# Pooling the first two batches' keys and values on TensorE, with a new lead-in order

## The chip, the cores and the metric

The kernel runs on one core of a Trainium2 chip. The metric is the device time of one execution in microseconds (us). Engines are named as in the profile: PE is TensorE (matmuls; PEld is its weight loads), DVE is VectorE, ACT is ScalarE, POOL is GpSimd, SP is SyncE, which issues the DMAs here.

## What is computed

Three stages follow one another on 4608 tokens (8 batches of 576): attention with keys and values averaged over groups of 8 rows, a SoLU layer with a normalization, and a SiLU layer.

```python
# q, k, v: (8 batches, 8 heads, 576, 64), f32
k_p = k.reshape(B, H, Sp, 8, D).mean(axis=3)        # Sp = 72
v_p = v.reshape(B, H, Sp, 8, D).mean(axis=3)
scores = scale * np.matmul(q, k_p.transpose(0, 1, 3, 2))
attn = softmax(scores)
x = np.matmul(attn, v_p)                             # to (4608, 512)
h = x @ w_in                                         # moe: 512 -> 1024
solu = h * softmax(h)
ln = (solu - mean) / np.sqrt(var + 1e-06) * g_ln
x = ln @ w_out                                       # 1024 -> 512
h = x @ w_in2                                        # moe2: 512 -> 2048
out = (h * sigmoid(h)) @ w_out2                      # 2048 -> 512
```

## The kernel before

Tokens are worked in 36 tiles of 128. Attention and the SoLU layer run as a software pipeline over the tiles: one step per tile from step 6 on, in an order of letters (`STEP`), and a lead-in for the first tiles with an order written out by hand (`SCRIPT`). The SiLU layer follows, first its input product, then its output product; the change doesn't touch either.

The letters: `q` loads a tile of queries, `S` makes its scores (`scores`, L311) and the negated maximum on DVE (L320), `X` the softmax (ACT L329, POOL L339 and L345), `T` transposes the probabilities on PE and splits them into a high and a low part (`probs_T`, L364, L369), `A` attends one segment of 256 or 320 tokens (`attend`, L415), `H` is the hidden product of a tile (`hidden1`, L440; `Ht,f,k` one eighth of it), `M`, `E`, `Z` the SoLU and its normalization (L451, L458 and L459, L468 and on), `N` the transposes of the result (L487), `P` the output product (`project1`, L504 and L505). `Bn,u` advances the background work n times, taking up new items whose step is at most u.

Background work is a list of generators, sorted by step. It holds the preparation of keys and values (`prep_k`, `prep_v`, `prep_v_rest`) and of the SoLU weights. The weights come as 64-bit floats: `convert` loads them (L130), scales the high words on ACT (L138) and builds 32-bit floats in three DVE steps (L141, L142, L145); `load_split` then keeps a rounded part (ACT L155) and the rest (POOL L156). There are 8 such pieces of the input weights (`w1i`) and 8 of the output weights (`w1o`).

Keys and values of every batch are laid out on the host so that the 8 rows of a group lie next to each other in a partition. `prep_k` loads a head pair (L236) into one of three shared buffers `raw`, sums the 8 on DVE (L241) and copies the halves into the block-diagonal `kbd` (ACT L246 for batches 0 and 1, POOL L248 later). `prep_v` does the same with the first 64 pooled rows (L256, L261), and splits them into `vbh` (ACT L267) and `vbl` (POOL L268). `prep_v_rest` takes the last 8 pooled rows of each head (L273, L278), which come three times over from the host, and writes them with POOL through a mask into `vls` (L283, L287).

PE's order is the order in which the program is written (`manual_schedule`); the order of ACT, DVE, POOL and SP in these stages is that of a planner, which goes by its own costs and by the program's order. `gps` gives PSUM buffers from a ring of 4.

Of the kernel before, what the change touches and what calls it, by code (L numbers as in the profile page):

```python
# [9 lines left out]
F32 = mybir.dt.float32  # L10
# [3 lines left out]
AF = mybir.ActivationFunctionType  # L14
# [6 lines left out]
POOL = 8  # L21
# [29 lines left out]
NRING = 9  # L51
UNITS = ((0, 1, 2), (3,), (4, 5), (6, 7))
LEAD = 5
EARLY = [4, 5, 6, 7, 9]
W1O, CH0, FIRST = 5, 7, 6
SCRIPT = """
q1 q0 S0 B6,-9 X0 B1,-8 B2,5 S1 B3,-8 q2 B1,2 q3 X1 B2,5 B3,-7 T0 T1 S2 X2 B2,-7 B2,-6 T2
B2,-7 B1,-7 S3 q4 B1,-7 q5 A0 H0,0,0 B1,-6 X3 H0,0,3 B1,2 B1,-7 B3,-7 H0,0,2 S4 B1,9 B6,2
H0,1,3 H0,0,1 H0,1,2 H0,1,0 X4 B1,5 T3 H0,1,1 B1,-6 B1,-7 B1,-6 q6 B2,2 M0 B1,5 E0 B1,-7 S5
Z0 B2,-7 T4 B4,2 H1,0,2 B7,2 A1 B2,5 B1,-7 B1,9 X5 B2,-6 H1,0,0 H1,1,2 H1,0,1 H1,1,1 H1,1,0  # L60
H1,0,3 B3,9 B2,-6 H1,1,3 M1 N0 T5 E1 Z1
"""
STEP = "B2 S H0 A B1 H1 M B1 B1 N E P1 X B3 P T B5 p B1 q B2 Z B1 B2"
TAIL = "H0 A H1 p B2 M N B1 E B2 Z P1 B2 B6 P B2"
# [18 lines left out]
def pooled_attention__solu__silu_kernel(  # L83
    ctx: ExitStack,
    tc: tile.TileContext,
    qT: bass.AP,
    kT: bass.AP,
    vm: bass.AP,
    vl: bass.AP,
# [103 lines left out]
    for i in range(2):  # L193
        nc.gpsimd.memset(kbd[i], 0.0)
        nc.gpsimd.memset(vbh[i].bitcast(F32), 0.0)
        nc.gpsimd.memset(vbl[i].bitcast(F32), 0.0)

    todo, going, ready = [], [], set()
    kept = {"s": 0, "p": 0, "x": 0}

    def add(step, key, items):
        todo.extend((step, key, x) for x in items)
        todo.sort(key=lambda x: x[0])
# [25 lines left out]
                    break  # L229

    raw_t, kp_t, vp_t, vr_t = {}, {}, {}, {}

    def prep_k(b, p):
        assert b < 2 or kept["s"] >= (b - 1) * S
        raw = aw.tile([P, SP, POOL], F32, tag="raw", name="raw", bufs=RAWS)
        nc.sync.dma_start(raw, kT[b, :, p])  # L236
        yield
        if p == 0:
            kp_t[b] = aw.tile([P, NP, SP], F32, tag="kp", name="kp", bufs=1)
        kp, kb = kp_t[b], kbd[b % 2]  # L240
        nc.vector.reduce_sum(kp[:, p], raw, axis=AX)  # L241
        yield
        for e in range(2):
            r = slice(64 * e, 64 * e + 64)
            if b <= 1:
                nc.scalar.activation(kb[r, p, e * SP : (e + 1) * SP], kp[r, p], AF.Copy)  # L246
            elif p == NP - 1:
                nc.gpsimd.tensor_scalar(  # L248
                    kb[r, :, e * SP : (e + 1) * SP], kp[r], 1.0, 0.0, op0=ALU.mult, op1=ALU.add
                )  # L250

    def prep_v(b, p):
        assert b < 2 or kept["x"] >= (b - 1) * S
        i = b % 2
        raw = aw.tile([P, SP, POOL], F32, tag="raw", name="raw", bufs=RAWS)[:, :D]
        nc.sync.dma_start(raw, vm[b, :, p])  # L256
        yield
        if p == 0:
            vp_t[b] = aw.tile([P, NP, D], F32, tag="vp", name="vp", bufs=1)
        vp = vp_t[b]  # L260
        nc.vector.reduce_sum(vp[:, p], raw, axis=AX)  # L261
        yield
        if p == NP - 1:
            for e in range(2):
                r = slice(64 * e, 64 * e + 64)
                hi, lo = vbh[i][r, :, r], vbl[i][r, :, r]
                nc.scalar.activation(hi, vp[r], AF.Copy)  # L267
                nc.gpsimd.tensor_tensor(lo, vp[r], hi.bitcast(F32), op=ALU.subtract)  # L268

    def prep_v_rest(b, g):  # L270
        i = b % 2
        raw = aw.tile([P, SP, POOL], F32, tag="raw", name="raw", bufs=RAWS)[0:96, :D]
        nc.sync.dma_start(raw, vl[b, :, g])  # L273
        yield
        if g == 0:
            vr_t[b] = aw.tile([96, 2, D], F32, tag="vlp", name="vlp", bufs=1)
        vp = vr_t[b]
        nc.vector.reduce_sum(vp[:, g], raw, axis=AX)  # L278
        yield
        if g == 1:  # L280
            vh = aw.tile([96, 2, D], F32R, tag="vlh", name="vlh", bufs=1)
            nc.scalar.activation(vh, vp, AF.Copy)
            nc.gpsimd.tensor_tensor(  # L283
                vh[32:64], vp[32:64], vh[32:64].bitcast(F32), op=ALU.subtract
            )
            for j in range(4):
                nc.gpsimd.tensor_scalar(  # L287
                    vls[i][:, j // 2 :: 2, (j % 2) * D : (j % 2 + 1) * D],
                    vh.bitcast(F32), mask[:, j : j + 1], 0.0, op0=ALU.mult, op1=ALU.add,
                )  # L290
# [690 lines left out]
    def batch_v(b):  # L981
        return [prep_v(b, p) for p in range(NP)] + [prep_v_rest(b, g) for g in range(2)]

    for b in range(1, B):
        j = b // 2
        k0, v0 = (9 * j + 1, 9 * j + 3) if b % 2 else (9 * j - 4, 9 * j - 2)
        for p in range(NP):
            add(k0 + p // 2, ("k", b), [prep_k(b, p)])
        for n, x in enumerate(batch_v(b)):
            add(v0 + n // 2, ("v", b), [x])  # L990
# [36 lines left out]
    def lead_in(script):  # L1027
        for word in script.split():
            what, n = word[0], [int(x) for x in word[1:].split(",") if x]
            if what == "q":  # L1030
                load_q(*n)
            elif what == "S":
                scores(*n)
            elif what == "X":
# [219 lines left out]
```

## Time and profile before

| what | value |
|---|---|
| median of 3 runs | 1362.82 us (1362.54 to 1364.48) |
| the profiled execution | 1365.19 us |
| its span, first to last instruction | 1363.4 us |
| mean granted TensorE clock | 0.975 of full speed |
| PE busy | 1280.6 us |
| DVE busy | 942.7 us |
| ACT busy | 745.8 us |
| POOL busy | 525.3 us |

The busy times are sums over the span. The stages differ: the first 100 us or so are the lead-in and the first steps, until about 600 us the attention and SoLU pipeline runs, and then the SiLU layer.

### The profile page before, as it was taken

Reading aid. Unit: us, or ns where it says so; the run is one execution under the profiler, and the core shown is the slowest. Engines: PE = TensorE matmul, PEld = TensorE weight load, DVE = VectorE, ACT = ScalarE, POOL = GpSimd, SP = SyncE. Lnnn points to the kernel's source line nnn. Section 1 sums busy time; section 2 is a strip of 40 time slices with the busy share of each in tenths; the row PEclk is TensorE's granted clock in tenths of the full one; section 3 lists DMA queues with packets and bytes.
Section 4 is the critical chain, followed back from the end, with each engine's and each line's share of the span. In section 5 each row is a group of like instructions: output and inputs, shape, how many; then the busy total and the mean of one; then the engine's idle time right before and its main releaser. Section 6 shows DMA issues by size and latency. Waiting matters only on the chain.

```text
span 1363.4 us, 22872 instructions
## 1 busy us (share of the span) xinstructions
PE 1280.6 (94%) x8136; PEld 1199.1 (88%) x8136; DVE 942.7 (69%) x1423; ACT 745.8 (55%) x1914; POOL 525.3 (39%) x728
## 2 busy tenths in 40 slices
PE   2579899989999989998999999999999999999998
PEld 2468787878888878887999999999999999999998
DVE  6997567777767665755866666656447887787775
ACT  4675555655655645544666667666544444444342
POOL 5565344344444334332423433333114333343332
PEclk9789999989999989999999999999999999999999
DMA  7645244443443320312577788666895333443421
GB/s 233 202 147 190 82 140 147 130 149 109 121 125 101 108 77 32 123 48 91 204 282 286 250 293 310 235 237 224 332 358 205 115 103 124 156 155 124 154 93 64
DMA packets 108226, 226.94 MB, mean 166 GB/s; under 512 B 9808, under 2 KB 43600, under 8 KB 106576
## 3 DMA queue, kind: packets, MB, share of 16 engines
q1 hardware_dynamic: 104080, 210.80, 46.5%
q10 hardware_dynamic: 4032, 14.68, 2.8%
q8 instruction: 64, 1.05, 0.3%
q14 instruction: 50, 0.41, 0.1%
HBM read 141.56 MB, written 83.89 MB: 165 GB/s over the span
## 4 chain that ended last, share of the span: by engine, by line
PE 61%; DMA 3%; DVE 2%; ACT 2%; POOL 0%; issue 0%; SPq 0%; ACTq 0%; DVEq 0%; POOLq 0%
PE op L928 27%; PE m L710 22%; PE hp L440 4%; PE xp L504 4%; PE xp L505 2%; DMA gd<-ga 1%; PE tp L487 1%; DMA gr<-gd 1%; DMA w2r<-w2if 1%; PE av L415 1%; PE sp L311 1%; DVE w2s L525 1%; DMA x2d<-xo 0%; ACT w2s L561 0%; ACT pr L329 0%
## 5 line engine op out<-in xcount | busy, mean ns | idle before, releaser
L710 PE MATMUL m<-t,w2s 128*128 128x384 f32 x2016 | 355.9, 337 | 12.3 <-ACT u L795 8.0
L710 PEld LDWEIGHTS m<-t,w2s 128*128 128x128 f32 x2016 | 353.0, 190 | 14.9 <-ACT u L795 9.0
L928 PE MATMUL op<-w2o,gt 128*128 128x256 f32 x3024 | 363.0, 283 | 0.0
L928 PEld LDWEIGHTS op<-w2o,gt 128*128 128x128 f32 x3024 | 363.0, 192 | 0.0
L504 PE MATMUL xp<-ln,w1oh 128*128 128x512 f32 x576 | 212.2, 408 | 2.0 <-DVE ln L124 1.9
L525 DVE TENSOR_TENSOR gt<-gr,gt 128x512 fp32r<-128x512 f32 x180 | 165.3, 952 | 68.6 <-ACT gt L905 68.6
L905 ACT ACTIVATE gt<-gr 128x512 fp32r<-128x512 f32 x180 | 103.4, 623 | 149.5 <-DVE gr L525 123.3
L505 PE MATMUL xp<-ln,w1ol 128*128 128x256 f32 x576 | 163.7, 284 | 0.0
L504 PEld LDWEIGHTS xp<-ln,w1oh 128*128 128x128 f32 x576 | 110.3, 192 | 26.9 <-DVE ln L124 2.8
L440 PE MATMUL hp<-w1ih,xTh 128*128 128x512 f32 x288 | 120.2, 417 | 8.2 <-DVE e L459 8.2
L440 PE MATMUL hp<-w1il,xTh 128*128 128x512 f32 x288 | 116.7, 405 | 0.6 <-POOL w1il L156 0.6
L884 POOL TENSOR_TENSOR s<-gr 128x512 f32<-128x512 f32 x36 | 57.8, 1605 | 153.8 <-DMA gr<-gd 81.0
L440 PE MATMUL hp<-w1ih,xTl 128*128 128x512 f32 x288 | 116.6, 405 | 0.0
L329 ACT ACTIVATE pr<-sp,st 128x72 f32<-128x72 f32 x288 | 88.0, 331 | 49.9 <-POOL st L321 49.7
L505 PEld LDWEIGHTS xp<-ln,w1ol 128*128 128x128 f32 x576 | 111.2, 193 | 0.1
L440 PEld LDWEIGHTS hp<-w1ih,xTh 128*128 128x128 f32 x288 | 57.0, 198 | 21.1 <-issue 8.2
L905 ACT ACTIVATE gt<-s 128x512 fp32r<-128x512 f32 x72 | 42.4, 622 | 55.2 <-POOL s L525 52.3
L721 DVE TENSOR_TENSOR gb<-m,u 128x384 f32<-128x384 f32 x48 | 26.7, 556 | 63.0 <-ACT u L775 55.1
L525 POOL TENSOR_TENSOR tt<-x2r 128x768 f32<-128x768 f32 x22 | 44.0, 2002 | 63.3 <-DMA x2r<-x2d 57.7
L440 PEld LDWEIGHTS hp<-w1ih,xTl 128*128 128x128 f32 x288 | 56.3, 196 | 13.2 <-DVE xTl L124 0.6
L440 PEld LDWEIGHTS hp<-w1il,xTh 128*128 128x128 f32 x288 | 56.9, 198 | 11.4 <-POOL w1il L156 0.9
L123 ACT ACTIVATE ln<-tp 128x512 fp32r<-128x512 f32 x72 | 39.3, 596 | 49.5 <-PE tp L487 49.3
(136 smaller groups left out, 2196.7 us busy)
## 6 DMA issues: line engine op xcount, KB each, us to landing
gr<-gd SPq DMA_DIRECT2D x48, 512.0 KB, 6.0
x2r<-x2d SPq DMA_DIRECT2D x12, 1536.0 KB, 7.5
gd<-ga SPq DMA_DIRECT2D x96, 192.0 KB, 2.5
gd<-gb SPq DMA_DIRECT2D x48, 384.0 KB, 3.1
wod<-wo SPq DMA_DIRECT2D x56, 256.0 KB, 2.4
gr<-gd SPq DMA_DIRECT2D x48, 256.0 KB, 5.3
q<-qT SPq DMA_DIRECT2D x36, 256.0 KB, 3.2
raw<-kT SPq DMA_DIRECT2D x32, 288.0 KB, 3.7
```

Source lines behind the costliest of these rows:

```text
L123: nc.scalar.activation(hi, src, AF.Copy)
L311: nc.tensor.matmul(sp[done : done + n, p // 2, (p % 2) * 2 * SP : (p % 2 + 1) * 2 * SP], q[:, p, done : done + n], kbd[b % 2][:, p, :], st ...
L329: behind["ACT"] = nc.scalar.activation(pr[:, g, h], sv[:, g, h], AF.Exp, scale=SCALE, bias=st[:, 0, g, h : h + 1], accum_out=st[:, 1, g, h ...
L440: nc.tensor.matmul(hp[:, f], l, r, start=(n == 1 and m == 0), stop=(n == KC and m == 2))
L504: nc.tensor.matmul(xp, w1oh[:, k, cs], ln[:, k], start=(k == 0), stop=False)
L505: nc.tensor.matmul(xp[:, :GW], w1ol[:, k, cs], ln[:, k, 0], start=False, stop=(k == FC1 - 1))
L525: eng.tensor_tensor(dst, a, b, op=ALU.subtract)
L710: nc.tensor.matmul(to, wt[:, a, o : o + P], tk[:, b, k], start=(start and k == 0 and m == 0), stop=(k == 1 and m == 2), skip_group_check=n ...
L721: eng.tensor_tensor(dst, a, b, op=ALU.add)
L884: nc.gpsimd.tensor_tensor(s1, a21, a22, op=ALU.add)
L905: nc.scalar.activation(ring[n][:, 0], src, AF.Copy)
L928: nc.tensor.matmul(op[:, 256 * h : 256 * h + 256], t[:, l, i, ts], w[:, r], start=(s == i == h == m == 0), stop=(s == NSET - 1 and i == h ...
```

## The change

Keys and values of batches 0 and 1 (`NATURAL = 2`) come from the host in natural rows: `kn` and `vn`, 576 rows of 512 columns a batch. `load_k` and `load_v` bring them into buffers that later hold other tiles (`ln`, `xo`, `e`): 128 rows to a partition set, so that the 8 rows of a group lie in 8 neighbouring partitions. `taps` holds zeros and ones: `every8` sums 8 partitions to one column, `slide` shifts it for accumulation into 64 rows, `last8` is for the last 8 pooled rows. `pool_k` makes 20 matmuls, with the raw rows as stationary operand, and copies the result out of PSUM into `kbd`. `pool_v` makes 8 accumulating matmuls and 4 for the last rows, with the raw rows as moving operand, and splits the result out of PSUM with ACT and DVE. The lead-in's order is new, with four more letters: `k`, `v` load, `K`, `V` pool. The first values are pooled behind the second tile's scores, ahead of the third tile's; the first segment's attention stands ahead of the third tile's transposes. Batches 2 to 7 are prepared as before, from arrays that now begin with batch 2. A cut of the diff:

```diff
+NATURAL = 2
...
 SCRIPT = """
-q1 q0 S0 B6,-9 X0 B1,-8 B2,5 S1 B3,-8 q2 B1,2 q3 X1 B2,5 B3,-7 T0 T1 S2 X2 B2,-7 B2,-6 T2
-B2,-7 B1,-7 S3 q4 B1,-7 q5 A0 H0,0,0 B1,-6 X3 H0,0,3 B1,2 B1,-7 B3,-7 H0,0,2 S4 B1,9 B6,2
-H0,1,3 H0,0,1 H0,1,2 H0,1,0 X4 B1,5 T3 H0,1,1 B1,-6 B1,-7 B1,-6 q6 B2,2 M0 B1,5 E0 B1,-7 S5
-Z0 B2,-7 T4 B4,2 H1,0,2 B7,2 A1 B2,5 B1,-7 B1,9 X5 B2,-6 H1,0,0 H1,1,2 H1,0,1 H1,1,1 H1,1,0
-H1,0,3 B3,9 B2,-6 H1,1,3 M1 N0 T5 E1 Z1
+q0 k0 q1 v0 K0 S0 B1,-7 X0 S1 B1,-7 V0 X1 q2 B1,-7 T0 T1 B1,-7 S2 B2,-7 k1 X2 q3 B2,-6 A0 T2 B2,-6
+H0,0,0 H0,0,1 S3 K1 v1 H0,0,2 X3 H0,0,3 q4 B3,-6 H0,1,0 S4 H0,1,1 X4 T3 H0,1,2 q5 H0,1,3 M0 B2,5
+V1 E0 S5 Z0 B2,5 X5 T4 H1,0,0 H1,0,1 A1 H1,0,2 H1,0,3 B3,5 H1,1,0 H1,1,1 H1,1,2 H1,1,3 M1 q6 B3,5
+N0 T5 E1 Z1 B3,9
 """
...
+    taps = wk.tile([P, 512], F32, tag="sqd", name="taps", bufs=1)
+    nc.gpsimd.memset(taps, 0.0)
+    slide, last8 = taps[:, 0:112], taps[0:64, 112:496].rearrange("p (j r i k) -> p j r i k", j=4, r=3, k=8)
+    every8 = slide[:, 48:64]
+    nc.vector.reduce_sum(every8, ident.rearrange("p (j k) -> p j k", k=8), axis=AX)
+    for j in range(4):
+        nc.gpsimd.tensor_scalar(
+            last8[:, j, :, j], every8[0:64, 0:8].rearrange("p (o k) -> p o k", o=1).to_broadcast([64, 3, 8]),
+            1.0, 0.0, op0=ALU.mult, op1=ALU.add,
+        )
...
+    def load_rows_of(src, b, to):
+        for j in (0, 2):
+            nc.sync.dma_start(
+                to(j, 2), src[b, j * P : (j + 2) * P].rearrange("(j p) d -> p j d", p=P)
+            )
+        nc.sync.dma_start(to(4, 1)[0:64, 0], src[b, 4 * P : S])
+
+    def load_k(b):
+        nat[b] = wk.tile([P, 8, 512], F32, tag="ln", name="nat")
+        load_rows_of(kn, b, lambda j, n: nat[b][:, j : j + n])
+
+    def load_v(b):
+        late = wk.tile([P, 2, 512], F32, tag="e" if b else "xo", name="natv", bufs=2 if b else 1)
+        head = nat[b]
+        nat["v", b] = [head[:, 5], head[:, 6], late[:, 0], late[:, 1], head[0:64, 7]]
+        nc.sync.dma_start(head[:, 5:7], vn[b, 0 : 2 * P].rearrange("(j p) d -> p j d", p=P))
+        nc.sync.dma_start(late, vn[b, 2 * P : 4 * P].rearrange("(j p) d -> p j d", p=P))
+        nc.sync.dma_start(head[0:64, 7], vn[b, 4 * P : S])
+
+    def pool_k(b):
+        kp = gps("kp")[:, : NP * SP].rearrange("p (a k) -> p a k", k=SP)
+        for j in range(5):
+            rows = P if j < 4 else 64
+            for p in range(NP):
+                nc.tensor.matmul(
+                    kp[:, p, 16 * j : 16 * j + rows // 8],
+                    nat[b][0:rows, j, p * P : (p + 1) * P], every8[0:rows, 0 : rows // 8],
+                    start=True, stop=True,
+                )
+        for e in range(2):
+            r = slice(64 * e, 64 * e + 64)
+            to = kbd[b % 2][r, :, e * SP : (e + 1) * SP]
+            if e == 0 or b:
+                nc.scalar.activation(to, kp[r], AF.Copy)
+            else:
+                nc.vector.tensor_copy(to, kp[r])
+        ready.add(("k", b))
+
+    def pool_v(b):
+        i = b % 2
+        vt = nat["v", b]
+        vp = gps("vp")[:, : NP * D].rearrange("p (a d) -> p a d", d=D)
+        for e in range(2):
+            r = slice(64 * e, 64 * e + 64)
+            for j in range(4):
+                nc.tensor.matmul(
+                    vp[r], slide[:, 48 - 16 * j : 112 - 16 * j],
+                    vt[j].rearrange("p (a e d) -> p e a d", e=2, d=D)[:, e],
+                    start=(j == 0), stop=(j == 3),
+                )
+        vr = gps("vr")[0:96]
+        for j in range(4):
+            nc.tensor.matmul(
+                vr.rearrange("p (g j d) -> p j g d", g=2, d=D)[:, j],
+                last8[:, j].rearrange("p r i k -> p (r i k)"),
+                vt[4].rearrange("p (g j d) -> p j g d", g=2, d=D)[:, j],
+                start=True, stop=True,
+            )
+        for e in range(2):
+            r = slice(64 * e, 64 * e + 64)
+            split(vbh[i][r, :, r], vbl[i][r, :, r], vp[r])
+        to = vls[i].rearrange("p a n -> p (a n)")
+        nc.scalar.activation(to, vr, AF.Copy)
+        nc.vector.tensor_tensor(
+            to[32:64], vr[32:64], to[32:64].bitcast(F32), op=ALU.subtract
+        )
+        ready.add(("v", b))
...
         for e in range(2):
             r = slice(64 * e, 64 * e + 64)
-            if b <= 1:
-                nc.scalar.activation(kb[r, p, e * SP : (e + 1) * SP], kp[r, p], AF.Copy)
-            elif p == NP - 1:
+            if p == NP - 1:
...
-    for b in range(1, B):
+    for b in range(NATURAL, B):
...
+            elif what in "kvKV":
+                {"k": load_k, "v": load_v, "K": pool_k, "V": pool_v}[what](*n)
...
-    add(-9, ("k", 0), [prep_k(0, p) for p in range(NP)])
-    add(-8, ("v", 0), batch_v(0))
...
+        "kn": c(k[:NATURAL].transpose(0, 2, 1, 3).reshape(NATURAL, S, DM)),
+        "vn": c(v[:NATURAL].transpose(0, 2, 1, 3).reshape(NATURAL, S, DM)),

```

## Rows read from the trace of the kernel before

**Rows 1.** Page, busy us, share of the span and instructions of each engine.
```profile
PE 1280.6 (94%) x8136; PEld 1199.1 (88%) x8136; DVE 942.7 (69%) x1423; ACT 745.8 (55%) x1914; POOL 525.3 (39%) x728
```

**Rows 2.** Windows: busy us and instructions of each engine in a stretch, granted clock, DMA.
```profile
30.00:40.00 10.00, 0.00 (x0) 0.00 (x0) 9.87 (x12) 5.00 (x23) 5.21 (x7) 0.59 0.55 186
...
0.00:85.30 85.30, 42.08 (x188) 33.62 (x189) 67.24 (x105) 50.86 (x177) 47.77 (x82) 0.86 0.63 202
...
0.00:112.50 112.50, 67.03 (x314) 54.31 (x314) 93.99 (x151) 74.37 (x248) 70.28 (x119) 0.88 0.61 193
...
160.00:300.00 140.00, 131.12 (x728) 112.47 (x728) 100.29 (x177) 81.33 (x276) 60.08 (x132) 0.96 0.43 129
```

**Rows 3.** Waits, 0 to 112 us: total us, times, longest.
```profile
PE pm L364 <- POOL pb L339: 23.0, 5, 13.0
...
PE sp L311 <- ACT kbd L246: 10.1, 2, 9.7
```

**Rows 4.** Groups by line, DVE, 0 to 81 us: busy us, mean ns; idle before.
```profile
L145 DVE SCALAR_TENSOR_TENSOR w<-raw,w 128x512 int32<-128x512 int32 x11 | 12.0, 1094 | 0.1
...
L142 DVE SCALAR_TENSOR_TENSOR w<-w,sign 128x512 int32<-128x512 int32 x12 | 10.7, 892 | 1.4 <-ACT w L138 1.2
...
L141 DVE TENSOR_SCALAR sign<-raw 128x512 int32<-128x512 int32 x12 | 9.1, 759 | 1.9 <-DMA raw<-w1i 1.9
...
L241 DVE TENSOR_REDUCE kp<-raw 128x72 f32<-128x576 f32 x12 | 8.8, 745 | 8.0 <-DMA raw<-kT 8.0
...
L261 DVE TENSOR_REDUCE vp<-raw 128x64 f32<-128x512 f32 x8 | 5.2, 673 | 1.6 <-DMA raw<-vm 1.6
...
L278 DVE TENSOR_REDUCE vlp<-raw 96x64 f32<-96x512 f32 x4 | 2.7, 664 | 0.0
```

**Rows 5.** Timeline, DVE, POOL and PE, 23 to 52 us: start, us, instruction.
```profile
23.52 0.68 DVE L142 SCALAR_TENSOR_TENSOR w<-w,sign 128x512 int32<-128x512 int32 x1
...
28.61 1.84 POOL L287 TENSOR_SCALAR vls<-vlh,mask 96x128 fp32r<-96x128 f32 x4
...
28.83 0.68 DVE L145 SCALAR_TENSOR_TENSOR w<-raw,w 128x512 int32<-128x512 int32 x1
...
29.43 3.75 DVE L141 TENSOR_SCALAR sign<-raw 128x512 int32<-128x512 int32 x1
...
30.42 2.48 POOL L156 TENSOR_TENSOR w1il<-w,w1ih 128x512 fp32r<-128x512 f32 x2
...
38.94 0.41 DVE L141 TENSOR_SCALAR sign<-raw 128x512 int32<-128x512 int32 x1
...
41.64 1.11 PE L364 MATMUL pm<-ident,pb 128*128 128x128 f32 x4 [12.96 <-POOL pb L339]
...
51.89 0.42 DVE L124 TENSOR_TENSOR xTl<-av,xTh 128x256 fp32r<-128x256 f32 x1
```

**Rows 6.** Groups by line, POOL, 0 to 81 us.
```profile
L268 POOL TENSOR_TENSOR vbl<-vp,vbh 64x256 fp32r<-64x256 f32 x4 | 3.4, 858 | 0.1
...
L287 POOL TENSOR_SCALAR vls<-vlh,mask 96x128 fp32r<-96x128 f32 x8 | 3.3, 422 | 0.2
...
L283 POOL TENSOR_TENSOR vlh<-vlp,vlh 32x128 fp32r<-32x128 f32 x2 | 1.3, 648 | 0.2
```

**Rows 7.** Timeline, PE, 25 to 86 us.
```profile
25.15 1.11 PE L364 MATMUL pm<-ident,pb 128*128 128x128 f32 x4 [4.05 <-POOL pb L339]
...
26.63 2.05 PE L311 MATMUL sp<-kbd,q 128*128 128x144 f32 x8
...
79.43 1.03 PE L487 MATMUL tp<-ident,e 128*128 128x128 f32 x8
...
80.95 1.15 PE L311 MATMUL sp<-kbd,q 128*128 128x144 f32 x8
...
85.30 0.47 PE L440 MATMUL hp<-w1ih,xTh 128*128 128x512 f32 x1 [3.20 <-DVE e L459]
```

**Rows 8.** Waits of the SP queue, 0 to 82 us.
```profile
SPq L256 <- DVE kp L241: 10.1, 6, 4.1
```

More of the change, by code (lines that the diff above doesn't have):

```diff
@@ L86, in pooled_attention__solu__silu_kernel @@
     qT: bass.AP,
+    kn: bass.AP,
+    vn: bass.AP,
     kT: bass.AP,
@@ L231, in pooled_attention__solu__silu_kernel @@
     raw_t, kp_t, vp_t, vr_t = {}, {}, {}, {}
+    nat = {}
+    def load_rows_of(src, b, to):
[14 more added lines that the diff above has]
+        nc.sync.dma_start(head[0:64, 7], vn[b, 4 * P : S])
@@ L233, in prep_k @@
     def prep_k(b, p):
-        assert b < 2 or kept["s"] >= (b - 1) * S
+        assert kept["s"] >= (b - 1) * S
         raw = aw.tile([P, SP, POOL], F32, tag="raw", name="raw", bufs=RAWS)
-        nc.sync.dma_start(raw, kT[b, :, p])
+        nc.sync.dma_start(raw, kT[b - NATURAL, :, p])
         yield
@@ L252, in prep_v @@
     def prep_v(b, p):
-        assert b < 2 or kept["x"] >= (b - 1) * S
+        assert kept["x"] >= (b - 1) * S
         i = b % 2
         raw = aw.tile([P, SP, POOL], F32, tag="raw", name="raw", bufs=RAWS)[:, :D]
-        nc.sync.dma_start(raw, vm[b, :, p])
+        nc.sync.dma_start(raw, vm[b - NATURAL, :, p])
         yield
@@ L272, in prep_v_rest @@
         raw = aw.tile([P, SP, POOL], F32, tag="raw", name="raw", bufs=RAWS)[0:96, :D]
-        nc.sync.dma_start(raw, vl[b, :, g])
+        nc.sync.dma_start(raw, vl[b - NATURAL, :, g])
         yield
@@ L1226 @@
         "qT": c(qr.transpose(2, 0, 1, 3)),
-        "kT": c(k.reshape(B, NP, 2, SP, POOL, D).transpose(0, 2, 5, 1, 3, 4).reshape(B, P, NP, SP, POOL)),
-        "vm": c(vr[:, :, :, :64].transpose(0, 2, 3, 1, 5, 4).reshape(B, P, NP, D, POOL)),
+        "kn": c(k[:NATURAL].transpose(0, 2, 1, 3).reshape(NATURAL, S, DM)),
+        "vn": c(v[:NATURAL].transpose(0, 2, 1, 3).reshape(NATURAL, S, DM)),
+        "kT": c(
+            k[NATURAL:].reshape(B - NATURAL, NP, 2, SP, POOL, D).transpose(0, 2, 5, 1, 3, 4)
+            .reshape(B - NATURAL, P, NP, SP, POOL)
+        ),
+        "vm": c(
+            vr[NATURAL:, :, :, :64].transpose(0, 2, 3, 1, 5, 4).reshape(B - NATURAL, P, NP, D, POOL)
+        ),
         "vl": c(
             np.tile(
-                v.reshape(B, 2, 4, SP, POOL, D)[:, :, :, 64:].transpose(0, 2, 3, 1, 5, 4)
-                .reshape(B, 1, 32, 2, D, POOL), (1, 3, 1, 1, 1, 1),
-            ).reshape(B, 96, 2, D, POOL)
+                v[NATURAL:].reshape(B - NATURAL, 2, 4, SP, POOL, D)[:, :, :, 64:].transpose(0, 2, 3, 1, 5, 4)
+                .reshape(B - NATURAL, 1, 32, 2, D, POOL), (1, 3, 1, 1, 1, 1),
+            ).reshape(B - NATURAL, 96, 2, D, POOL)
         ),
```

## Prediction

> **What bounds the kernel now.** I read the profile from the whole to the part: first the engines' busy shares, then busy time by stage, then who waits for whom in the first 112 us, then the instructions of the engine that sets the pace there.
>
> TensorE (PE) is busy 94% of the span [rows 1], and from 160 us on it has 131.12 of 140 us [rows 2]: behind the lead-in nothing but less matmul work would help, and the change takes none away there. In the lead-in it is otherwise. Until 85.30 us, when the first matmul of the third tile's hidden layer starts [rows 7], PE is busy 42.08 us and idle 43.2; VectorE (DVE) is busy 67.24 [rows 2]. From 30 to 40 us PE does nothing at all while DVE is busy 9.87 of 10; from 85.30 to 112.50 DVE is busy 93.99 - 67.24 = 26.75 of 27.2 us [rows 2]. So where the lead-in loses time, DVE is full.
>
> The waits say the same in another form. PE's largest waits are for the probabilities (23.0 us, the longest 13.0) and for the first keys (10.1, of which 9.7 before the first matmul) [rows 3]. POOL writes the probabilities, but they are late because the maximum of that tile stood behind weight conversions on DVE: one `sign` operation there lasts 3.75 us against 0.41 for the same shape elsewhere, while POOL works on the values [rows 5]. The waits end on POOL, ACT or DVE by name; the queue that is full is DVE's.
>
> **What is removed.** Both batches' pooling reductions leave DVE: 8 of keys at 0.745 us, 8 of values at 0.673 and 4 of the last value rows at 0.664 (the key group of [rows 4] has 12 because 4 belong to batch 2 and stay): 5.96 + 5.38 + 2.66 = 14.0 us. POOL loses the low halves and the masking of the values of both batches, 3.4 + 1.3 + 3.3 = 8.0 us [rows 6].
>
> That POOL work also costs DVE. Undisturbed, the three steps of a conversion last 0.41, 0.68 and 0.68 us [rows 5]; in the lead-in they took 9.1 - 12 x 0.41 = 4.2, 10.7 - 12 x 0.68 = 2.5 and 12.0 - 11 x 0.68 = 4.5 us more than that [rows 4], 11.2 in sum. POOL is busy 47.77 us until 85.30 [rows 2], of which some 5 are the first microseconds' memsets, before any conversion. If the stall is spread over the other 43, the removed 8.0 take 8.0 / 43 x 11.2 = 2.1 us of it along; 0 and 8.0 (every removed microsecond stood in front of a conversion) are the ends.
>
> **What is added on DVE.** A copy of half the keys of batch 0, four subtractions for the low half of the values and two for the last rows, all out of PSUM, and one small reduction at the start. The nearest row is the 128x256 subtraction out of PSUM, 0.42 us [rows 5]: 0.45 for the 288-column copy, 4 x 0.42, 2 x 0.7 for 512 columns (in proportion 0.84, so a little under), 0.2: 3.7 us, at most 5. DVE's sum: -14.0 - 2.1 + 3.7 = -12.4 us, between -9 and -18.3.
>
> **What is added on PE.** A tile's scores are four matmuls in the code and 8 in the trace [rows 7]: each f32 matmul is two records. Pooled keys are 20 matmuls a batch, so 40 records, whose stationary operand is 128 columns of raw rows and whose moving operand is only 16 columns. The nearest row with as wide a load is the transpose, 1.03 / 8 = 0.13 us: 5.2 us. If the time went by moving columns, 16 / 144 of a score's record, it would be under 1 us; I take the load, which is what the two have in common. Pooled values are 8 matmuls of 256 columns and 4 of 128: 16 records at 1.15 / 8 x 256 / 144 = 0.25 and 8 at 0.13: 5.0 us. So 10.2 us a batch, 20.4 in all at the fast durations. The scores at 26.63 us ran slow, 2.05 / 8 = 0.26 us a record [rows 7]; at that price a batch is 10.4 + 9.5 = 19.9 and both are 40. I take slow to middling for batch 0 (15) and fast for batch 1 (10): 25 us.
>
> They cost nothing as long as they lie in PE's idle 43.2 us. What hides them: the keys of batch 0 run piece by piece as their rows land, in the 9.7 us in which PE waits now; the values of batch 0 run while the softmax of the first two tiles is on ACT and POOL (PE idles 4.05 us ahead of the second tile's transposes [rows 7]); keys and values of batch 1 fall into waits for weights and for the read of the hidden tile. 42 + 25 + 6 us before the first rows are there give 73 us as PE's own bound for the moment that is now 85.30, if no other wait were left: at most 12 us earlier.
>
> **What is moved.** Queue SP: raw rows come in whole into buffers of their own, 3 transfers for the keys and 3 for the values of a batch instead of 4 and 6 that share three buffers. The 10.1 us in which value transfers held the SP queue until DVE had read keys [rows 8] go, and with them the weights queued behind. Bytes: keys 1.18 MB as before, values 1.18 instead of 1.44, so 0.5 MB less. The order puts the first attention ahead of the third tile's transposes: in the kernel before it comes behind the transposes that wait until 41.64 us. More output-weight conversions stand ahead of the second tile's normalization in program order (seven chunks against four); that delays the third hidden tile by up to 3 x 2 us and is work that the next stretch then lacks. The first scores may start 0 to 3 us later than now, since 40 loads replace four reductions; DVE waits there anyway. Later batches keep their pooling, and the loops behind the lead-in are the same.
>
> **The sum.** DVE gives 12.4 us back and PE allows 12 at most. Some of DVE's saving falls where DVE already waits (18 us until 85.30, most of it in the first 30); a fifth lost to that leaves 10. Behind the lead-in the same steady loop follows, so a lead-in that ends 10 us earlier ends the kernel 10 us earlier. The profiled execution took 1365.19 us, 1.8 around its span; it becomes 1355. That execution was 2.4 us above the median of the runs shown, 1362.82, so the forecast for the median is 1353.
>
> **A rule weighed.** DVE's 3.75 us `sign` stands against 0.41, with POOL's masking of values and then a weight's low half beside it [rows 5]; the row shows that they block each other, the groups show 11.2 us of it in sum [rows 4]. The Trainium skill, SBUF — State Buffer, section "Who interferes with whom", says that GpSimd and a VectorE operation in a two-port mode or with two SBUF inputs share one port pair, and that the later one is fully blocked, not slowed. By that rule, read strictly, each removed POOL microsecond frees up to one of DVE and the saving is 18.3 instead of 12.4; by the spread over rows it is 12.4. The trace agrees on blocking, but POOL is busy 47.77 us against 11.2 of stall, so most POOL time blocks nobody.
>
> **The rivals.**
> Forecast: DVE's relief carries, 3 to 14 us faster, 1349 to 1360: chance 0.58.
> More: the removed POOL work was just what stalled DVE (the end of 8.0 above), and PE runs fast throughout. For it: the longest stall lies beside it. Against: PE's 12 us bound, which only falls if matmuls that are slow now become fast. 16 us, 1347: chance 0.13. That is the rule above.
> Nothing: PE's in-order queue takes back what DVE gives. PE waits for values of batch 0 or 1 with the scores behind them, and the lead-in ends as now; or the conversions of output weights, still all to be done before the first projection, set the end. For it: 16 chunks at 2 us and more are DVE's largest block and stay. 1360 to 1365, within 0.2%: chance 0.15.
> Slower: the pooling runs at the slow durations, 40 us on PE. Its place is ahead of the second scores and the transposes, where the chain of tiles is serial. 42 + 40 + 6 = 88 us before any wait, plus 5 that stay, is 93 against 85.30: 8 us slower, 1371. It decides when PE's added work exceeds 85.3 - 42 - 6 - 5 = 32 us. Against: with the pauses filled, PE should not be slow for so long; the same scores took 1.15 us at 80.95 [rows 7]. Chance 0.14.
>
> **How the numbers follow.** Faster by more than 0.2% (2.7 us, about what a measurement of this kernel can tell from no change) is 0.58 + 0.13 = 0.71; same 0.15; slower 0.14. The range from 1346 to 1364 holds the forecast, the case of nothing and most of the case of more, and leaves out the slower case and a little at the fast end.
>
> **What would show it.** In the changed profile: no reduction of raw rows on DVE before those of batch 2; DVE's busy time until the third hidden tile down by some 10 us; key pooling at about 0.13 us a record once PE is fast; the wait for probabilities, now 23.0 us, less than half; the third hidden tile's first matmul near 75 us; the stretch from 160 us on with the same busy share. Wrong it would be if that matmul comes at 75 us and the end doesn't move (the gain given back in the projections), or if PE shows new waits for raw values.

## The result, and the profile after

The changed kernel takes 1374.37 us (median of 4 runs, 1372.36 to 1374.84) against 1362.68 for the kernel before (4 runs): ratio 1.0079, 95% interval 1.006 to 1.0098, so 11.7 us slower. The prediction, 1353 and at most 1364, was wrong in sign. The profiled execution took 1374.43 us, its span 1372.6. A trace is one execution, up to some 6 us from its kernel's median (1359.51 us against 1365.61 for batch 1 alone in the new order, 1373.22 against 1368.03 with less matmul work, both below), and from the first projection to the end the traced executions of all kernels here take 1247 to 1259 us, so ends are compared by medians and traces are read for places in the lead-in.

The work went where it was sent. The page of the changed kernel, engine line (as [rows 1]): DVE has 10.9 us less than before, PE 14.6 more.

```profile
PE 1295.2 (94%) x8264; PEld 1214.9 (89%) x8264; DVE 931.8 (68%) x1411; ACT 743.9 (54%) x1901; POOL 519.6 (38%) x719
```

Windows of the changed kernel (columns as in [rows 2]); the stretches beyond those of before end at the third tile's first hidden matmul (95.00) and at the first projection (118.12):

```profile
0.00:16.74 16.74, 8.79 (x41) 8.68 (x41) 1.70 (x6) 2.24 (x4) 4.81 (x18) 1.00 0.89 311
...
40.00:58.00 18.00, 16.95 (x82) 14.63 (x83) 12.38 (x19) 8.58 (x28) 8.72 (x10) 0.62 0.64 217
0.00:85.30 85.30, 61.00 (x308) 52.13 (x309) 55.00 (x94) 47.90 (x162) 41.98 (x70) 0.84 0.64 210
0.00:95.00 95.00, 62.25 (x317) 53.19 (x317) 64.61 (x107) 55.49 (x176) 47.62 (x77) 0.84 0.63 204
0.00:112.50 112.50, 75.39 (x376) 63.87 (x377) 77.89 (x128) 64.87 (x205) 60.12 (x102) 0.85 0.60 195
0.00:118.12 118.12, 81.01 (x410) 68.94 (x411) 81.02 (x138) 68.97 (x230) 61.39 (x104) 0.86 0.60 192
160.00:300.00 140.00, 133.59 (x754) 115.44 (x753) 97.55 (x173) 80.82 (x277) 60.28 (x134) 0.96 0.42 125
```

In the kernel before, the first projection came at 106.87, and this is its window:

```profile
0.00:106.87 106.87, 61.41 (x282) 49.45 (x283) 88.65 (x141) 70.47 (x241) 65.24 (x107) 0.87 0.63 198
```

Read the DVE column (third busy figure). Up to the first projection DVE works 81.02 us instead of 88.65, and stands idle 118.12 - 81.02 = 37.1 us instead of 106.87 - 88.65 = 18.2. It was relieved, and the relief turned into waiting. From 160 us on PE is as full as before, and the first projection is already 11.25 us late: the loss is made ahead of that. The conversions on DVE aren't what is late: the third step of the last output-weight conversion starts at 97.56 us, 102.45 before.

```profile
97.56 0.67 DVE L147 SCALAR_TENSOR_TENSOR w<-raw,w 128x512 int32<-128x512 int32 x1
```
```profile
102.45 1.02 DVE L145 SCALAR_TENSOR_TENSOR w<-raw,w 128x512 int32<-128x512 int32 x1
```

Where the chain of tiles falls behind is seen in the timeline of PE, ACT and DVE of the changed kernel, 5 to 66 us (more rows of before are in [rows 5, 7]):

```profile
5.62 8.78 PE L271 MATMUL kp<-taps,nat 128*128 128x16 f32 x40 [5.62 <-DMA nat<-kn]
...
14.49 1.28 ACT L280 ACT_TABLE_LOAD   x1 [14.49 <-PE kp L271]
15.79 0.40 ACT L280 ACTIVATE kbd<-kp 64x288 f32<-64x288 f32 x1
...
16.22 0.46 DVE L282 COPY kbd<-kp 64x288 f32<-64x288 f32 x1 [2.71 <-ACT kbd L280]
...
16.74 3.63 PE L391 MATMUL sp<-kbd,q 128*128 128x144 f32 x16 [2.33 <-DVE kbd L282]
...
20.30 1.08 PE L292 MATMUL vp<-nat,taps 128*64 128x256 f32 x4
...
41.05 1.11 PE L444 MATMUL pm<-ident,pb 128*128 128x128 f32 x4 [5.69 <-POOL pb L419]
...
46.98 5.56 PE L271 MATMUL kp<-taps,nat 128*128 128x16 f32 x40
...
52.48 0.79 PE L520 MATMUL hp<-w1ih,xTh 128*128 128x512 f32 x1
...
65.30 1.25 PE L391 MATMUL sp<-kbd,q 128*128 128x144 f32 x8
```

and, in the kernel before, ACT and PE from 7 to 107 us:

```profile
7.77 1.28 ACT L246 ACT_TABLE_LOAD   x1 [7.77 <-DVE kp L241]
...
9.69 1.92 PE L311 MATMUL sp<-kbd,q 128*128 128x144 f32 x6 [9.69 <-ACT kbd L246]
...
61.48 1.25 PE L311 MATMUL sp<-kbd,q 128*128 128x144 f32 x8 [1.00 <-ACT pr L329]
...
106.87 0.48 PE L504 MATMUL xp<-ln,w1oh 128*128 128x512 f32 x1
```

The 40 records of key pooling run from 5.62 to 14.4, 0.22 us each. Behind them stand a table load of ACT and two copies, and the first scores start at 16.74 instead of 9.69. The table load is not new: in the kernel before it stood ahead of the first scores too, but it could start at 7.77, behind the first of four reductions, and now starts at 14.49, behind all 40 records. That is 6.72 of the 7.05 us. The new order then makes up for it: the third tile's probabilities are transposed at 41.05 instead of 41.64 [rows 7], and the first hidden product starts at 42.39 instead of 49.73. But from 41 us on PE is busy without a gap, at a granted clock of 0.62 between 40 and 58 us, and the keys of batch 1 stand in that stretch with 5.56 us more. What was won is gone behind it. PE reaches the values of batch 1 at 61.47 us, when the sixth tile's scores started before (61.48); it pools for 3.83 us, and those scores start at 65.30.

The timeline of the changed kernel from 83 to 119 us shows the loss at its largest:

```profile
83.87 1.03 PE L567 MATMUL tp<-ident,e 128*128 128x128 f32 x8
...
85.40 1.15 PE L391 MATMUL sp<-kbd,q 128*128 128x144 f32 x8
...
87.92 1.12 ACT L538 ACTIVATE e<-hp,ls 128x1024 f32<-128x1024 f32 x1
...
88.12 1.64 POOL L158 TENSOR_TENSOR w1ol<-w,w1oh 128x512 fp32r<-128x512 f32 x1 [4.74 <-ACT w1oh L157]
...
88.55 1.49 DVE L143 TENSOR_SCALAR sign<-raw 128x512 int32<-128x512 int32 x1
...
91.72 1.86 DVE L147 SCALAR_TENSOR_TENSOR w<-raw,w 128x512 int32<-128x512 int32 x1
91.78 1.25 POOL L158 TENSOR_TENSOR w1ol<-w,w1oh 128x512 fp32r<-128x512 f32 x1
...
93.62 1.23 DVE L539 SCALAR_TENSOR_TENSOR e<-hp,e 128x1024 f32<-128x1024 f32 x1
...
95.00 0.77 PE L520 MATMUL hp<-w1ih,xTh 128*128 128x512 f32 x1 [8.45 <-DVE e L539]
...
118.12 0.48 PE L584 MATMUL xp<-ln,w1oh 128*128 128x512 f32 x1
```

The first tile's normalization transposes are 4.4 us late (83.87 against 79.43), the third tile's hidden product 9.7 us (95.00 against 85.30): its wait for `e` on DVE grew from 3.20 to 8.45 us, behind conversions. The waits of PE in the changed kernel, 0 to 112 us, in sum (as [rows 3]):

```profile
PE pm L444 <- POOL pb L419: 13.1, 4, 5.7
PE hp L520 <- DVE e L539: 10.3, 2, 8.5
PE kp L271 <- DMA nat<-kn: 5.6, 1, 5.6
...
PE sp L391 <- DVE kbd L282: 2.3, 1, 2.3
```

### The profile page after: what moved, and what is told of

It is laid out like the page before. It is cut to its first block, busy times and chain, and to the rows that moved or that the text cites. A ratio compares the mean times of both kernels' runs of the same rounds, so it can differ in the third digit from the quotient of the medians.

```text
span 1372.6 us, 23084 instructions
## 1 busy us (share of the span) xinstructions
PE 1295.2 (94%) x8264; PEld 1214.9 (89%) x8264; DVE 931.8 (68%) x1411; ACT 743.9 (54%) x1901; POOL 519.6 (38%) x719
## 4 chain that ended last, share of the span: by engine, by line
PE 58%; DMA 4%; DVE 3%; ACT 3%; POOL 1%; issue 1%; SPq 0%; ACTq 0%; DVEq 0%; POOLq 0%
PE op L1008 26%; PE m L790 21%; PE hp L520 4%; PE xp L584 3%; PE xp L585 1%; DMA gd<-ga 1%; DMA w2r<-w2if 1%; DMA gr<-gd 1%; PE tp L567 1%; PE av L495 1%; ACT pr L409 1%; DMA x2d<-xo 1%; DVE w2s L605 0%; DMA gd<-gb 0%; DVE e L539 0%
## 5 line engine op out<-in xcount | busy, mean ns | idle before, releaser
L520 PE MATMUL hp<-w1ih,xTh 128*128 128x512 f32 x288 | 119.8, 416 | 12.2 <-DVE e L539 12.2
L605 POOL TENSOR_TENSOR s<-s,gr 128x512 f32<-128x512 f32 x36 | 52.2, 1451 | 35.8 <-DVE gr L605 26.3
```

The source lines that it names most:

```text
L520: nc.tensor.matmul(hp[:, f], l, r, start=(n == 1 and m == 0), stop=(n == KC and m == 2))
L605: eng.tensor_tensor(dst, a, b, op=ALU.subtract)
```

## Experiments

Each was timed beside the kernel before on its chip (medians there 1362.9 to 1364.1 us). "Late" is what the median has above that. Letters are those of the order.

### The two halves of the change

The new order with the old pooling on DVE, and pooling on PE in the old order:

```diff
-q1 q0 S0 B6,-9 X0 B1,-8 ...                 # e1, on the kernel before
+q0 q1 K0 S0 B1,-7 X0 S1 ...                 # the new order; K and V only
+elif what in "KV": need(what.lower(), n[0]) # wait for prep_k, prep_v
-q0 k0 q1 v0 K0 S0 B1,-7 X0 S1 ...           # e2, on the change: the old order
+q0 k0 q1 K0 S0 B6,-9 X0 v0 B1,-8 ... T0 T1 S2 V0 X2 ...
+... H0,0,2 K1 S4 ... T4 B4,2 V1 H1,0,2 ...
```

> The new lead-in order with the old pooling on DVE (the words K and V stand for the point where the preparation must be done; the words k and v are left out). Theory price (the pooling matmuls themselves lie on the path: 8.8 us ahead of the first scores, 9.4 us in a stretch where PE is full): the order costs nothing, the time stays within 3 us of the kernel before, 1360 to 1366. Theory order (the third tile's transposes ahead of the first hidden tile, and seven output-weight conversions ahead of the second tile's normalization): 8 us or more slower than before, 1371 and up.

> Natural rows and pooling on PE as in the change, but the order of the kernel before, with the eight new words put in: keys 0 ahead of the first scores, values 0 behind the third scores, keys 1 ahead of the fifth scores, values 1 ahead of the second hidden tile. Theory price: slower than before as the change is, 1370 to 1376. Theory order: DVE's relief shows, 1352 to 1360.

The order alone: 1368.88, ratio 1.0039 (1.0024 to 1.0054), 4.8 us late. Pooling alone: 1374.44, 1.0069 (1.0045 to 1.0093), 10.3 us late. The order alone lies between its two theories, the pooling alone at the theory of the price. Neither half helps, and the pooling has the larger loss, though the two intervals overlap. In the order alone the third tile's transposes come at 34.15, 7.5 us ahead of before, and the first tile's normalization transposes at 77.32, 2.1 ahead; the lead is lost behind that, the fourth tile's come 5.8 us late. With pooling in the old order the first tile's are 12.1 us late already.

### The keys of batch 0

Batch 0's keys back on DVE, the rest as in the change; and the change with 24 more records on PE ahead of the pooling:

```diff
-K0: pool_k(0)                               # e8
+K0: need("k", 0)      # prep_k(0, p), kT holds batch 0 again
-q0 k0 q1 v0 K0 S0                           # e3
+W12 q0 k0 q1 v0 K0 S0 # W: 12 matmuls of ident by ident
```

> The change with the keys of batch 0 alone pooled as before (laid out by group, summed on DVE, copied by ACT); all else as in the change. Theory start (the 40 slow records ahead of the first scores shift everything behind them): first scores back at 9 to 11 us, the first normalized tile 5 us earlier, the end 4 to 6 us earlier than the change, 1368 to 1370. Theory queue (later queues set the end): first scores early, the end within 2 us of the change.

> The change with 12 more f32 matmuls of the identity on PE (24 records of 128 columns) before the first keys land, their result unused. Theory slow (the pooling costs what it does because the matmuls run at their slow durations after idle stretches): the 40 records of the first keys fall from 8.8 us to 5 or 6 and the first scores start at 13 to 14 us instead of 16.7; the end 2 to 4 us earlier than the change. Theory load (the records are slow for another reason, or the start is not what the end waits for): first scores at 16 to 18, the end within 2 us of the change.

Keys on DVE: 1367.3, 1.0033 (1.002 to 1.0047), 4.2 us late: some 7 of the 11.7 us are gone with this one part. The extra records: 1371.32, 1.0054 (1.0037 to 1.0071), 8.2 late: with work added to PE the median is some 3 us below the changed kernel's, though the two intervals overlap. Timeline of PE with the extra records:

```profile
1.86 5.23 PE L250 MATMUL warm<-ident 128*128 128x128 f32 x24 [1.86 <-POOL ident masks.py:199]
6.92 5.76 PE L276 MATMUL kp<-taps,nat 128*128 128x16 f32 x40
```

The same 40 records take 5.76 instead of 8.78 us. So their time, not the landing of the rows, held the first scores in the change. Starting 1.3 us later themselves, they bring the scores only 1.6 us forward (15.14), and with the keys on DVE the scores of the first two tiles end at 17.73 instead of 20.37, 2.6 us sooner. Both have more than that in the median. With the keys on DVE the fifth tile's scores start at 51.78 against 56.61 in the change, 4.8 us sooner, and the first projection comes at 113.81 against 118.12, 4.3 sooner; the rest of the 7 us arises behind the lead-in and isn't read. One reading of what is gained by the fifth tile is the next place where PE is full; windows of 40 to 60 us, the changed kernel and that with the keys on DVE:

```profile
40.00:60.00 20.00, 18.95 (x95) 16.25 (x95) 13.93 (x21) 8.61 (x29) 10.67 (x12) 0.66 0.59 198
```
```profile
40.00:60.00 20.00, 19.86 (x115) 15.96 (x115) 15.74 (x23) 11.39 (x45) 9.72 (x13) 0.85 0.63 212
```

PE is busy in both, with 95 matmuls in the one and 115 in the other, at granted clocks of 0.66 and 0.85; the 40 records of batch 1's keys take 5.56 and 4.63 us there. What shifts PE's clock in that stretch no run here isolates.

In the old order, with batch 0's keys on DVE and the other three poolings on PE, the loss is small too:

```diff
-q0 k0 q1 K0 S0 B6,-9 X0 v0                  # e11, against e2
+q1 q0 S0 B6,-9 X0 v0    # prep_k(0, p); V0 behind T0, K1 behind S2
```

> The old order with the first keys on DVE; values 0, keys 1 and values 1 on PE (values 0 behind the first transposes, keys 1 behind the third scores, values 1 ahead of the second attention). Theory start: at least 4 us faster than the old order with all pooling on PE (1374.4), 1366 to 1370; theory relief: faster than the kernel before, 1356 to 1361; theory idle: 1371 or more.

1366.53, 1.0023 (1.001 to 1.0035), 3.6 us late against 10.3 with those keys on PE too (the values of batch 0 and the keys of batch 1 also stand elsewhere there). Batch 1's keys lie here in PE's wait for the third tile's probabilities, and PE still waits behind them:

```profile
27.50 5.56 PE L282 MATMUL kp<-taps,nat 128*128 128x16 f32 x40
...
43.47 1.12 PE L460 MATMUL pm<-ident,pb 128*128 128x128 f32 x4 [10.40 <-POOL pb L435]
```

In this place idle time is room: the transposes come at 43.47, 1.8 us later than in the kernel before.

### Less matmul work

The kernel leaves out most of the rows in the sums of pooled keys and values, so its result is not the pooled one; it serves for the time alone.

```diff
-for j in range(5): 4 matmuls each           # e5: keys 20 -> 4 a batch
+4 matmuls of 64 rows x 72 columns
-for j in range(4): 2 matmuls each           #     values 8 -> 2 a batch
+for j in range(3, 4): ...
```

> The change with most of the pooling matmuls left out: keys take 4 matmuls a batch instead of 20 (only the last 64 rows are summed), values 2 + 4 instead of 8 + 4 (only the last full block of rows); everything else stays. Theory price: 8 to 12 us faster than the change, 1362 to 1366, the first scores at 8 to 10 us instead of 16.7. Theory order: at most 3 us faster, 1371 and up.

1368.03, 1.0049 (1.0026 to 1.0072), 3.9 us late, between the two theories. The first scores start at 15.83, only 0.9 sooner, since the last block of rows lands at 9.54 and the copies follow; yet by the medians 7.8 of the 11.7 us are gone. The two intervals overlap, so this only suggests that the first scores alone don't carry the loss and that the poolings behind them pay too.

### The conversions ahead of the third hidden tile

The wait of 8.45 us looks like the loss itself, so the conversions were moved behind `E1`; `E1` was moved ahead of them; and from `M0` on the old order was put in:

```diff
-M0 B2,5 V1 E0 S5 Z0 B2,5 X5 ... H1,0,3 B3,5 H1,1,0 ... q6 B3,5 N0 T5 E1 Z1 B3,9
+M0 V1 E0 S5 Z0 X5 ... N0 T5 E1 B2,5 Z1 B2,5 B3,5 B3,5 B3,9     # e4
-M1 q6 B3,5 N0 T5 E1 Z1 B3,9
+M1 E1 q6 N0 T5 B3,5 Z1 B3,9                                    # e6
-M0 B2,5 V1 E0 S5 ...                                           # e7
+M0 B1,5 E0 B1,-7 S5 q6 Z0 B2,-7 T4 ... # as before, V1 ahead of A1
```

> The change, with the background words that bring the output-weight conversions moved behind the second tile's normalization. Theory order: PE's wait of 8.45 us for the second tile's read by DVE falls to 3 or 4 and the kernel is 4 to 6 us faster than the change, 1368 to 1370. Theory price: the third hidden tile may start earlier, but all eight conversions still stand ahead of the first projection, and the end moves by 2 us at most, 1372 to 1376.

> The change with one move: the second tile's SoLU (its exponential on ACT and its product on DVE) stands ahead of the last two groups of background words and of the transposes. Theory queue (that read stands behind weight conversions on DVE, and the time lost there stays lost): PE's wait of 8.45 us before the third hidden tile falls to 3 to 4 and the kernel is 4 to 5 us faster than the change, 1369 to 1370. Theory sum (the conversions must all be done before the first projection, so what is gained there is lost behind it): within 2 us of the change, as the kernel with late output weights suggests.

> The change with the new order up to the first hidden tile and the order of the kernel before from there on (first maximum to second normalization). Theory order (the loss between the first and the third normalized tile, 9.2 us with pooling on DVE, 6.8 in the change, 0.4 with the old order, comes from the second half of the order): the lag against the kernel before stays at 4 to 6 us after the first normalized tile, the end at 1367 to 1369. Theory sum: within 2 us of the change, 1372 to 1376.

All slower than the change or no better: 1378.37 (1.0115, 1.0098 to 1.0131), 1378.34 (1.0113, 1.0089 to 1.0137) and 1375.56 (1.0093, 1.0069 to 1.0117). Timeline of PE with `E1` first:

```profile
89.57 0.47 PE L520 MATMUL hp<-w1ih,xTh 128*128 128x512 f32 x1 [2.04 <-DVE e L539]
...
98.34 1.23 PE L567 MATMUL tp<-ident,e 128*128 128x128 f32 x8 [3.07 <-POOL e L555]
...
111.80 1.12 PE L444 MATMUL pm<-ident,pb 128*128 128x128 f32 x4 [12.22 <-POOL pb L419]
```

The wait shrank to 2.04 us and the third hidden tile came at 89.57, and then a wait of 12.22 us for probabilities stands 22 us further on. Taking the named wait away brought nothing back: it is a place where lateness shows. The theory that the time is lost there fell.

### Batch 1 alone on PE

Batch 0 as before on DVE and POOL, only batch 1 pooled on PE: in the new order; in the old one in the gap ahead of the third tile's probabilities, with its loads ahead of weights; in the old one as late as its use allows, its loads behind the weights; and in the new order up to `M0` with the old one behind:

```diff
-k0 v0 K0 V0                                 # e10: prep_k(0, p), batch_v(0)
-q3 X1 ... S2 X2                             # e9, old order
+q3 k1 v1 X1 ... S2 K1 V1 X2
-q5 A0 ... H0,0,2 S4 B1,9 ... T4 B4,2 H1,0,2 # e15, old order
+q5 k1 A0 ... H0,0,2 K1 S4 B1,9 v1 ... T4 B4,2 V1 H1,0,2
-M0 B2,5 V1 E0 ...                           # e16: e10, then the old order
+M0 B1,5 E0 B1,-7 S5 q6 Z0 B2,-7 T4 B4,2 H1,0,2 B7,2 V1 A1 ...
```

> The change with batch 0 back on DVE, keys and values; batch 1 on PE as in the change. Theory start (the pooling ahead of the first two tiles is what costs): as the kernel with the first keys on DVE or better, 1364 to 1368. Theory idle: pooling of batch 1 in PE's full stretch still costs its 9.4 us there, 1369 or more, no faster than the new order with all pooling on DVE (1368.9).

> The kernel before, with batch 1 alone from natural rows and pooled on PE, in the 13 us in which PE waits for the third tile's probabilities; batch 0 on DVE, the old order otherwise. It takes 7 us of reductions off DVE between 36 and 60 us, where DVE is full. Theory relief (DVE's time is worth time where DVE is full and PE idle): 3 to 7 us faster than the kernel before, 1356 to 1360. Theory idle (DVE's saved time comes back as DVE waiting, since the chain of tiles through PE, ACT and POOL sets the pace): within 2.7 us of the kernel before, or slower.

> The old order and the old pooling for batch 0; only batch 1 is pooled on TensorE, at the places where its values are first needed (keys ahead of S4, values ahead of A1), its loads issued just before A0 and behind S4, behind the weights. Theory 'the serial head pays': nothing stands on PE ahead of the first scores or the first attention, the first scores stay near 9 us, and the relief of DVE by batch 1 is kept: 1360 to 1363, at or a little below the kernel before. Rival 'any piece on PE ahead of the tiles delays them, whichever order': slower by 3 to 8 us, 1366 to 1371, with a new wait of S4 for the copy of the keys or of A1 for the values.

> As the run with batch 0 on DVE and batch 1 on TensorE in the new order (1365.6), but from M0 on with the old order of letters. Theory 'the new order loses its 5 us in the tail, where the third hidden tile waits for the normalization': 1361 to 1363. Rival 'the loss of the order lies in its head (the conversions put late), and the tail only shows it': 1365 to 1368, no better than the run with the whole new order.

New order: 1365.61, 1.002 (1.0002 to 1.0037), 2.7 us late, the smallest ratio of all kernels tried; against the order alone (4.8 late) pooling batch 1 on PE may be worth some 2 us there, though the two intervals overlap. Old order: 1374.58, 1.0096 (1.0069 to 1.0122), and late in the old order 1376.32, 1.0103 (1.0083 to 1.0123): 11.7 and 12.7 us late for the same matmuls. New head, old tail: 1367.63, 1.0033 (1.002 to 1.0046), 4.0 late: the old tail brings nothing back.

The late one shows the mechanism most plainly. Timeline of PE, window of that stretch, and a wait of DVE until 125 us, in that kernel:

```profile
52.72 8.64 PE L282 MATMUL kp<-taps,nat 128*128 128x16 f32 x40
61.29 3.15 PE L407 MATMUL sp<-kbd,q 128*64 128x144 f32 x16
```
```profile
52.72:61.30 8.58, 8.58 (x42) 8.52 (x40) 0.00 (x0) 0.00 (x0) 1.39 (x2) 0.50 0.19 71
```
```profile
DVE st L416 <- PE sp L407: 12.1, 2, 11.8
```

and the same window in the kernel before:

```profile
52.72:61.30 8.58, 7.14 (x41) 5.19 (x39) 7.06 (x12) 4.66 (x22) 5.60 (x8) 1.00 0.71 215
```

For 8.58 us PE pools keys, and DVE and ACT do nothing at all; before, DVE was busy 7.06 of the same stretch. The scores that the pooling stands ahead of start at 61.29 instead of 53.49, and DVE's reduction of them waits 11.8 us; what stands behind it in DVE's order is late with it (the third step of the last output-weight conversion starts at 113.79 us, 102.45 before). Some 4 us of the delay go with PE's clock: in the new order the same 40 records took 4.63 us at a granted clock of 1.00, and DVE was busy 4.11 us beside them. Timeline of PE and window, batch 1 in the new order:

```profile
40.08 4.63 PE L281 MATMUL kp<-taps,nat 128*128 128x16 f32 x40
```
```profile
40.08:44.71 4.63, 4.63 (x43) 4.58 (x41) 4.11 (x7) 0.00 (x0) 0.80 (x2) 1.00 1.02 332
```

With the loads early, in the old order, the pooling lies in the gap but its transfers stand ahead of weights: PE waits 7.0 us for a converted weight. So there the loss seems to come by the loads; no run separates the two.

### Conversions earlier, hidden work ahead of the transposes

```diff
-A0 T2 B2,-6 H0,0,0 H0,0,1 S3                # e12: e10 with
+A0 B2,-6 H0,0,0 H0,0,1 T2 S3
-q4 B3,-6 ... S4 H0,1,1 X4 T3 H0,1,2 q5      # e13: e12 with
+q4 B3,5 ... S4 B2,5 H0,1,1 X4 T3 B1,5 H0,1,2 q5 B1,5   # and W1O = 4 for 5
                                             # e14: the change with both
```

> Batch 0 on DVE, batch 1 on PE, the new order (1365.6) with one move: the first two eighths of the first hidden tile ahead of the third tile's transposes, for whose probabilities PE waits 5 us. Theory chain (PE's serial order sets the pace up to the first normalized tile): that tile comes 2 to 4 us earlier, and the end 1 to 4 us earlier. Theory conversions (DVE's read of the second hidden tile behind weight conversions sets the end): the first normalized tile earlier, the third as before, the end within 2 us.

> As the kernel with the hidden tile first, and the output-weight conversions brought up instead of later, into the stretch from 50 to 60 us in which DVE is busy 4.2 of 10 in the change. Theory conversions: PE's wait for the read of the second hidden tile (7.9 us in the kernel with batch 1 on PE) falls to 3 or 4, the end 3 to 6 us earlier than without, 1358 to 1362. Theory chain: no earlier than the kernel with the hidden tile first alone.

> The change itself, all four poolings on PE, with the same two moves (first hidden eighths ahead of the third transposes, output-weight conversions earlier). Theory conversions: 4 to 8 us faster than the change, 1366 to 1370, with the 5 to 7 us of the late first scores left. Theory chain: 1 to 3 us faster, 1371 to 1373.

1367.6 (1.0025, 1.0009 to 1.0041), 1373.82 (1.0076, 1.0061 to 1.0091) and 1382.52 (1.0139, 1.0123 to 1.0155). The hidden work ahead of the transposes gains nothing (3.6 us late, 2.7 without it). Conversions put earlier cost 6 us with batch 0 on DVE; both moves on top of the change, which were expected to gain 1 to 8 us, cost 7. With the conversions put later (e4, e6) the medians are 4 us above the change's, put earlier they cost too: no move of them gave time back.

## Why the prediction was wrong

**The step that failed** is the cover for the matmuls added: "They cost nothing as long as they lie in PE's idle 43.2 us", with its instance, the keys of batch 0 "in the 9.7 us in which PE waits now", and the sentence that followed from it, first scores "0 to 3 us later ...; DVE waits there anyway". The sum of PE's idle time was taken for room. It lies between steps of one chain, scores, softmax, transposes, attention, hidden product, and a pooling put into PE's order ahead of a step of that chain that is ready delays the step by its length (the sixth scores start 3.82 us late, behind 3.83 us of values). The keys' records began with the first rows, but they took 8.78 us, and the first scores came 7.05 us later, not 0 to 3; putting those keys back on DVE gave some 7 us at the end. That DVE waits there was true, and was the reason for concern: its idle time until the first projection grew by 18.9 us, more than the work it lost.

**What bounds the kernel.** "Where the lead-in loses time, DVE is full" held for the rows shown, yet didn't say that relief of DVE is time at the end. The late batch 1 took pooling off DVE too, and ended 12.7 us late.

**DVE's sum** came out near: forecast -12.4 us, between -9 and -18.3. Over the whole execution 942.7 became 931.8, -10.9, close to the pieces without the stall, -14.0 + 3.7 = -10.3, so of the 2.1 us of stall little shows. (Until 85.30 us 67.24 became 55.00, -12.2, but in that window some work of before is late.) The added pieces were priced well; four groups of DVE in the changed kernel, 0 to 95 us, make 3.9 us against 3.7:

```profile
L126 DVE TENSOR_TENSOR vbl<-vp,vbh 64x256 fp32r<-64x256 f32 x4 | 1.7, 420 | 0.1
...
L310 DVE TENSOR_TENSOR vls<-vr,vls 32x512 fp32r<-32x512 f32 x2 | 1.4, 684 | 0.9 <-ACT vls L309 0.8
...
L282 DVE COPY kbd<-kp 64x288 f32<-64x288 f32 x1 | 0.5, 461 | 2.7 <-ACT kbd L280 2.7
L204 DVE TENSOR_REDUCE taps<-ident 128x16 f32<-128x128 f32 x1 | 0.3, 286 | 2.3 <-POOL taps L201 2.3
```

**PE's sum** was near too: 25 us forecast; 8.78 + 3.9 for batch 0 and 5.56 + 3.83 for batch 1 make 22.1 (PE's total grew by 14.6, so its other matmuls took less time in this execution). Taking the load of 128 columns as the price, not the 16 moving columns, was the better choice.

**The milestones.** Third hidden tile near 75 us: 95.00. Key pooling at about 0.13 us a record once PE is fast: 0.22 for batch 0, 0.14 for batch 1 (5.56 / 40). Wait for probabilities under half of 23.0: 13.1, a little over. Conversions ahead of the second normalization: their delay was seen ("up to 3 x 2 us") and the wait grew by 5.25 us, but taking it away didn't help. The steady stretch behind: as forecast. The SP queue: by 82 us its 10.1 us behind key reductions of [rows 8] fell to 6.8, all for batch 2, but its waits for conversions' buffers grew from 23.5 to 35.4.

**The rivals.** "Slower" named the place, "ahead of the second scores and the transposes, where the chain of tiles is serial", and nearly the size, 1371; only its condition was wrong. It asked for over 32 us of added PE work, and 22 did it, since the place decides and not the sum. "More" fell. Its rule, from the Trainium skill, SBUF — State Buffer, section "Who interferes with whom" (the later of two is fully blocked), agrees with the row at 88.55: a `sign` that starts while POOL writes a low half (88.12 to 89.76) ends at 90.04 and takes 1.49 us against 0.42 elsewhere. The third step at 91.72 takes 1.86 against 0.68, but the low half beside it starts 0.06 us later, so which of the two is the later isn't clear there. What was freed didn't reach the end.

**What stays open.** The cost of pooling batch 0's keys on PE is shown by undoing it, and that a pooling in the chain delays it and idles DVE by the late batch 1. How 2.6 us at the first scores become 4.8 at the fifth and 7 at the end is only partly read (the granted clock from 40 to 60 us). Lags in the lead-in and in the median don't agree closely either: in the old order with batch 0's keys on DVE the first projection of the trace comes at 115.00 us, 8.1 late, and the median is 3.6 late; what happens behind the lead-in wasn't read. Why the new order alone costs 4.8 us isn't settled: in the runs with batch 1 on PE the new head with the old tail isn't faster, and moves of the conversions made things worse in both directions. That its head is at fault is only argued. The moves were tried on top of pooling on PE, not on the order alone. No version beat the kernel before.

## What to carry to other kernels

In this kernel idle time of an engine was room only for work that no step of the chain waits behind: before moving work to an engine that waits, name the instruction queued next in that engine's order, and whether it is on the chain. Price the moved work by its first use, here 8.78 us of matmuls ahead of the first copy, where the first of four reductions had been enough to start. And when a wait looks like the loss, take it away before believing it: here it came back 22 us later, larger.

## What the hardware showed

A matmul record with 128 stationary and 16 moving columns took 0.216 us in a stretch with a granted clock of 0.50 (1.2 GHz), 8.64 / 40, and 0.116 at 1.00 (2.4 GHz), 4.63 / 40. The first 40 records of the changed kernel took 0.22 each, like those at 0.50, though the granted clock reads 1.00 from 0 to 16.74 us; PE had done nothing before them. Behind 24 records of 128 columns they took 0.144. So by their durations these records ran at the lower level, and the clock's row doesn't show it there.

In the late batch 1 the granted clock read 0.50 for the whole 8.58 us of the 40 records, in which PE was busy throughout; from 40 to 52.72 us, ahead of them, PE had been busy 9.10 of 12.72 us at 0.92.
